# A linear-attention and GELU-MLP kernel: kv of a batch in one slot, batch 4 loaded before batch 2's x transposes, maps and casts behind the n slots

## The chip, the cores and the metric

One NeuronCore of a Trainium2 chip runs the kernel. The metric is device time in microseconds (us). TensorE does the matmuls, VectorE, ScalarE and GpSimd the elementwise work, and SyncE (SP) issues nearly all DMAs; ScalarE issues the output writes.

## What is computed

q, k and v have 8 batches, 8 heads, 576 positions and a head size of 64. Each head goes through linear attention; its output x (4608 x 512) goes through two matrices with a tanh GELU between.

```python
phi = lambda x: np.where(x > 0, x, np.exp(x) - 1.0) + 1.0
q_p, k_p = phi(q), phi(k)
kv  = np.einsum('bhsd,bhse->bhde', k_p, v)
z   = np.sum(k_p, axis=2)
x   = np.einsum('bhsd,bhde->bhse', q_p, kv) / (np.einsum('bhsd,bhd->bhs', q_p, z)[..., None] + 1e-06)
x   = x.transpose(0, 2, 1, 3).reshape(4608, 512)
out = gelu_tanh(x @ w_in) @ w_out          # w_in 512 x 2048, w_out 2048 x 512
```

## The kernel before

**Tiling.** Of a batch's 576 positions, 512 ("main", four chunks of 128) are done by themselves; the remaining 64 of two batches are one "rest" tile of 128. So there are nine iterations of the MLP: iteration j (0 to 7) takes the 512 tokens of batch j, iteration 8 the rest tokens of all batches. An iteration has 16 `h` steps (four matmuls of 128x512 each, then a GELU by ScalarE into `g`) and 16 `o` steps (four matmuls each; four o steps fill one output tile).

**phi.** exp(x) comes from ScalarE (`exp_of`), max(x + 1, 1) from VectorE (`linear_of`, L223), and the minimum of the two from VectorE (`least_of`, L236). v is cast to bf16 beside a column of ones (`cast_v` L247, `cast_v_paired` L241, `cast_vr` L255), so that one matmul gives kv and z.

**Attention of a batch.** kv is summed on TensorE (`kv_main`, 40 matmuls, or `kv_paired`, 36, for batches 0 and 1) and copied into the block-diagonal `kvbd` (`kv_evac`). For each chunk c, `n` multiplies the transposed q (`qt`) with kvbd into PSUM (`n_ps`), and VectorE forms a reciprocal (L315) and a product (L317) that gives x (`nab`; `nab_in_banks` does the same in two halves with banks of its own). x is transposed to `xt`, which the h matmuls of that batch's iteration read: for batches 0 and 1 by TensorE and a ScalarE copy, for the others by DMA transposes that SP issues (L576). phi(q) is transposed likewise, by four DMA transposes per batch (L545) from batch 2 on. Each h matmul reads all four chunks of xt.

**PSUM.** Six banks (`bank`) rotate over h, o, t_ps and others; `pair_of_banks` is one more pair, with one buffer, which n uses for each chunk in turn.

**Order.** Each engine runs its instructions in the order in which the program writes them, and so does SP with its DMAs; an instruction that has to wait holds up what stands behind it. The program writes an iteration as 32 slots, one per step, with the work on later batches put into slots by hand: `at(j, slot, fn)` runs fn after that step of iteration j. Iterations 0 and from 2 on have h in slots 0 to 15 and o in 16 to 31; iteration 1 has h in 0 to 7, the first half of all four o tiles in 8 to 15, h in 16 to 23 and the second half of o in 24 to 31. `plan_prepare(b, s_linear, s_exp)` places the maps of q and k in the slots s_linear and +1, the casts of v in +2, the exponentials in s_exp, the minimum of q with its four DMA transposes in s_exp + 2 and that of k in + 4. `plan_attention(b, j, s_kv, s_n)` places kv, its evacuation, and n with the DMA transpose of each chunk. `plan_rest` does the rest tile; `load_batch(b)` issues q, k, on even b the rests of k and v (two DMAs each, for two batches), and v. Loads go into seven buffers of 1 MB that are used in turn.

First batch (batch 0) and second batch (batch 1) have programs of their own: `first_batch`, ahead of iteration 0, and `plan_second`, in iteration 0's o slots.

Of the kernel before, what the change touches and what calls it, by code (L numbers as in the profile page):

```python
# [15 lines left out]
def kernel(  # L16
# [15 lines left out]
    nc = tc.nc  # L32
# [3 lines left out]
    P = 128  # L36
# [40 lines left out]
    def pair_of_banks(name):  # L77
        return ps_a.tile([P, 2, 512], FP32, name=name, tag="a")
# [161 lines left out]
    def cast_v_paired(b, us, fn):  # L240
        fn(  # L241
            out=vp_paired(b)[:, :, us, 0:D].rearrange("p j u d -> p u j d"),
            in_=ld["v", b][:, us].rearrange("p u (j d) -> p u j d", d=D),
        )
# [9 lines left out]
            r = slice(REST * s, REST * (s + 1))  # L254
            nc.vector.tensor_copy(out=vrs[s][r, :, 0:D], in_=ld["vr", m][r])  # L255

    def kv_paired(b, ii, kv_ps):
        kp, vp = phi["k", b], vp_paired(b)
        for j in range(J):
            for a in range(2):  # L260
                r = slice(HP * a, HP * (a + 1))
                nc.tensor.matmul(  # L262
                    kv_ps[:, a, 2 * E * ii : 2 * E * (ii + 1)],
                    lhsT=kp[r, j, 2 * ii : 2 * ii + 2, :],
                    rhs=vp[r, j, 2 * ii : 2 * ii + 2, :],
                    start=(j == 0),
                    stop=(j == J - 1),
                    skip_group_check=True,
                )
# [13 lines left out]
                    skip_group_check=True,  # L283
                )

    def kv_evac(b, src, fns):
        for s, fn in enumerate(fns):
            r = slice(HP * s, HP * (s + 1))
            dst = kvbds[b % 4][r, :, E * s : E * (s + 1)]
            if b in PAIRED:  # L290
                fn(
                    out=dst.rearrange("p (a i) e -> p a i e", a=2),
                    in_=src[r, :, 0 : 4 * E].rearrange("p a (i e) -> p a i e", i=2)[
                        :, :, :, E * s : E * (s + 1)
                    ],
                )
            else:
                fn(out=dst, in_=src[r])  # L298

    def nab_mm(qt_c, kvbd, ns, rows=slice(0, P)):  # L300
        for i in range(NP):
# [23 lines left out]
    def nab(qt_c, b):  # L325
        n_ps = pair_of_banks("n_ps")
        nab_mm(qt_c, kvbds[b % 4], [n_ps[:, a] for a in range(2)])
        return nab_evac(n_ps, b in PAIRED)
# [56 lines left out]
    def first_batch():  # L385
        w_ps = bank("w_ps", [P, 512])

        def keep_warm(n):
            for _ in range(n):
                nc.tensor.matmul(w_ps, lhsT=warm[:, 0:P], rhs=warm)  # L390

        qt = pt.tile([P, C, NP, P], BF16, name="qt")
        qs = (slice(0, 4), slice(4, 8))

        def transpose_q(s, fn):
            t_ps = bank("t_ps", [P, C, 2, P], BF16)
            for i in range(2):
                for c in range(C):
                    h = 4 * s + 2 * i
                    nc.tensor.transpose(  # L400
                        t_ps[:, c, i, :], phi["q", 0][:, c, h : h + 2, :], ident
                    )
            fn(out=qt[:, :, 2 * s : 2 * s + 2, :], in_=t_ps)

        keep_warm(18)
        for s in range(2):
            exp_of("q", 0, qs[s])
            exp_of("k", 0, halves[s])
            linear_of("q", 0, qs[s])
            least_of("q", 0, qs[s])  # L410
            linear_of("k", 0, halves[s])
            least_of("k", 0, halves[s])
        transpose_q(0, nc.vector.tensor_copy)
        keep_warm(10)
        transpose_q(1, nc.scalar.copy)
        cast_v_paired(0, halves[0], nc.vector.tensor_copy)
        cast_v_paired(0, slice(2, 3), nc.scalar.copy)
        cast_v_paired(0, slice(3, 4), nc.vector.tensor_copy)
        keep_warm(2)
        kv_ps = pair_of_banks("kv_ps")  # L420
        for ii in range(2):
            kv_paired(0, ii, kv_ps)
        kv_evac(0, kv_ps, (nc.vector.tensor_copy, nc.scalar.copy))
        gelu_table()
        for s in range(2):
            cast_w_in(0, nc.gpsimd.tensor_copy, slice(256 * s, 256 * s + 256))
        for i in range(1, 4):
            cast_w_in(i, nc.gpsimd.tensor_copy)
        for i in range(2):
            cast_w_out(i, nc.gpsimd.tensor_copy)  # L430
        cast_w_out(2, nc.gpsimd.tensor_copy, slice(0, 2))
        keep_warm(2)

        xts[0] = pt.tile([P, NP, MAIN], BF16, name="xt")
        x = {0: nab_in_banks(qt[:, 0], 0), 1: nab(qt[:, 1], 0)}
        for c in range(C):
            transpose_x(x[c], xt_chunk(0, c), nc.scalar.copy)
            if c + 2 < C:
                x[c + 2] = (nab_in_banks, nab)[c % 2](qt[:, c + 2], 0)
            if c > 0:  # L440
                h_quarter(0, c - 1, 3)
        h_quarter(0, C - 1, 3)
# [15 lines left out]
    def plan_second():  # L458
        b = 1
        x = {}  # L460

        def maps():
            for n in "qk":
                exp_of(n, b)
            gelu_table()
            for n in "qk":
                linear_of(n, b)
                least_of(n, b)
            cast_w_out(2, nc.vector.tensor_copy, slice(2, 4))

        def transpose_q():
            qts[b] = pt.tile([P, C, NP, P], BF16, name="qt")
            for s in range(2):
                t_ps = bank("t_ps", [P, 2, NP, P], BF16)
                for c in range(2):
                    for i in range(NP):
                        nc.tensor.transpose(
                            t_ps[:, c, i, :],
                            phi["q", b][:, 2 * s + c, 2 * i : 2 * i + 2, :],
                            ident,  # L480
                        )
                nc.scalar.copy(qts[b][:, 2 * s : 2 * s + 2], t_ps)

        def casts():
            cast_v_paired(b, halves[0], nc.vector.tensor_copy)
            cast_v_paired(b, halves[1], nc.scalar.copy)

        def kv():
            kv_ps = pair_of_banks("kv_ps")
            for ii in range(2):  # L490
                kv_paired(b, ii, kv_ps)
            kv_evac(b, kv_ps, (nc.vector.tensor_copy, nc.scalar.copy))
            cast_w_out(3, nc.scalar.copy, slice(0, 1))
            cast_w_out(3, nc.vector.tensor_copy, slice(1, 2))
            cast_w_out(3, nc.gpsimd.tensor_copy, slice(2, 4))

        def n(c):
            x[c] = nab(qts[b][:, c], b)

        def t(c):  # L500
            if c == 0:
                xts[b] = pt.tile([P, NP, MAIN], BF16, name="xt")
            transpose_x(x[c], xt_chunk(b, c), nc.scalar.copy)

        at(0, 15, maps)
        at(0, 23, transpose_q)
        at(0, 25, casts)
        at(0, 27, kv)
        at(0, 27, n, 0)
        at(0, 28, n, 1)  # L510
        at(0, 28, t, 0)
        at(0, 29, n, 2)
        at(0, 29, t, 1)
        at(0, 30, h_quarter, b, 0, 2)
        at(0, 30, n, 3)
        at(0, 30, t, 2)
        at(0, 31, h_quarter, b, 1, 2)
        at(0, 31, t, 3)
        at(0, 31, h_quarter, b, 2, 2)
        at(0, 31, h_quarter, b, 3, 2)  # L520
# [41 lines left out]
        at(j, s + 4, least_k)  # L562

    def plan_attention(b, j, s_kv, s_n):
        box = {}

        def kv(i):
            if i == 0:
                box["kv"] = bank("kv_ps", [P, NP, E])
            kv_main(b, i, box["kv"])  # L570

        def n(c):
            x = nab(qts[b][:, c], b)
            if c == 0:
                xts[b] = pt.tile([P, NP, MAIN], BF16, name="xt")
            nc.sync.dma_start_transpose(out=xt_chunk(b, c), in_=x)  # L576

        for i in range(NP):
            at(j, s_kv[i], kv, i)
        at(j, s_kv[-1], lambda: kv_evac(b, box["kv"], (nc.vector.tensor_copy,) * 2))  # L580
        for c in range(C):
            at(j, s_n[c], n, c)

# [110 lines left out]
    plan_second()  # L694
    plan_prepare(2, (1, 2), (1, 7))
    at(1, 7, gelu_table)
    plan_attention(2, 1, (16, 17, 18, 19), (20, 21, 23, 24))
    plan_prepare(3, (1, 11), (1, 23))
    plan_rest(0, 1, 23, 28, 2, 14)
    at(1, 23, gelu_table)  # L700
    at(1, 26, load_batch, 4)
    for b in range(4, B):
        plan_prepare(b, (b - 2, 8), (b - 2, 15))
        if b > 4:
            at(b - 3, 15, load_batch, b)
    for m in range(1, 4):
        at(2 * m - 1, 14, load_rest, "qr", q, m)
        plan_rest(m, 2 * m, 15, 22, 2 * m + 1, 14)
    for b in range(4, B):
        at(b - 2, 15, gelu_table)  # L710
    for b in range(3, B):
        plan_attention(b, b - 1, (1, 2, 3, 4), (6, 8, 10, 12))

    for j in range(B + 1):
        iteration(j)
# [30 lines left out]
```

## Time and profile before

| | |
|---|---|
| runs, median (lowest to highest) | 317.26 us (316.98 to 318.13) |
| profiled execution: time, span | 317.26 us, 315.5 us |
| busy share of the span: TensorE, VectorE, ScalarE, GpSimd | 91%, 34%, 52%, 6% |
| mean granted clock of TensorE | 0.984 |
| chain that ended last, by engine | PE 67%, DMA 13%, DVE 12%, ACT 3% |
| bytes moved, mean rate | 53.76 MB, 170 GB/s |

In the profile PE is TensorE's matmul queue, PEld its weight loads, DVE is VectorE, ACT ScalarE, POOL GpSimd, SPq and ACTq the instructions that issue DMAs. L302 is line 302 of the kernel. The chain that ended last is followed back from the last instruction, at each step to what released it. A busy share is a mean over stages with different limits, so the stages are to be read one by one.

### The profile page before, as it was taken

How to read it: one execution, taken by the hardware profiler on the slowest of the kernel's cores; microseconds unless marked ns; L12 is line 12 of the kernel's file. 1: busy time of each engine (PE TensorE's matmuls, PEld its weight loads, DVE VectorE, ACT ScalarE, POOL GpSimd, SP SyncE). 2: the span in 40 equal slices, each digit the busy share in tenths (PEclk: the TensorE clock that was granted, in tenths of full speed). 3: DMA queues.
4: the chain of work that ended last, by engine and by line, in shares of the span. 5: the costliest groups of instructions: out<-in, count | busy, mean ns of one | idle time of the engine just before them, and what ended most of it. 6: DMA issues, size and time to landing. Idle time of an engine off the chain costs nothing.

```text
span 315.5 us, 4408 instructions
## 1 busy us (share of the span) xinstructions
PE 287.8 (91%) x1796; PEld 138.1 (44%) x1796; DVE 108.1 (34%) x178; ACT 163.6 (52%) x221; POOL 18.4 (6%) x25
## 2 busy tenths in 40 slices
PE   8699978998997099999998799999999999999995
PEld 3364445444443044454443344444444444444444
DVE  3731448374625425064304650463032100200001
ACT  4666944783954048366634492558257146206600
POOL 5164310000000000000000000000000000000000
PEclk9999999999999679999999999999999999999999
DMA  7999998953399929915896299134402210011022
GB/s 262 409 406 402 407 359 271 369 134 67 68 215 320 166 50 320 262 54 66 273 312 132 50 328 273 30 57 95 155 19 50 85 66 0 19 66 66 0 64 71
DMA packets 71379, 53.76 MB, mean 170 GB/s; under 512 B 42048, under 2 KB 62784, under 8 KB 71360
## 3 DMA queue, kind: packets, MB, share of 16 engines
q1 hardware_dynamic: 68656, 44.58, 49.5%
q10 hardware_dynamic: 2704, 8.91, 8.6%
q8 instruction: 14, 0.23, 0.3%
q14 instruction: 5, 0.04, 0.1%
HBM read 36.70 MB, written 9.44 MB: 146 GB/s over the span
## 4 chain that ended last, share of the span: by engine, by line
PE 67%; DMA 13%; DVE 12%; ACT 3%; issue 2%; SPq 1%; DVEq 0%
PE o_ps L642 32%; PE h_ps L357 30%; DMA k_x<-in_k_dram 7%; DMA qt<-q_p 3%; DVE x L317 3%; DMA qtr<-qr_p 2%; PE n_ps L302 2%; DVE k_p L223 2%; DVE q_p L223 2%; PE kv_ps L277 1%; DVE vp L247 1%; ACT g L367 1%; DVE r L315 1%; DVE k_p L236 1%; PE kv_ps L262 1%
## 5 line engine op out<-in xcount | busy, mean ns | idle before, releaser
L642 PE MATMUL o_ps<-w_out_sb,g 128*128 128x512 bf16 (+1 forms) x592 | 127.1, 373 | 1.4 <-DVE w_out_sb L143 1.1
L357 PE MATMUL h_ps<-xt,w_in_sb 128*128 128x512 bf16 (+1 forms) x572 | 123.2, 360 | 2.2 <-ACT g L367 1.6
L367 ACT ACTIVATE g<-h_ps 128x512 bf16<-128x512 f32 x144 | 85.1, 597 | 71.3 <-PE h_ps L357 70.1
L642 PEld LDWEIGHTS <-g 128*128 128x128 bf16 x592 | 57.6, 98 | 66.7 <-issue 1.8
L357 PEld LDWEIGHTS <-w_in_sb 128*128 128x128 bf16 x636 | 56.6, 98 | 58.6 <-issue 3.9
L615 ACT COPY o_sb<-o_ps 128x512 f32<-128x512 f32 (+1 forms) x18 | 10.3, 574 | 60.1 <-PE o_ps L642 53.4
L613 DVE COPY o_sb<-o_ps 128x512 f32<-128x512 f32 (+1 forms) x19 | 12.8, 675 | 59.5 <-PE o_ps L642 59.5
L302 PE MATMUL n_ps<-kvbd,qt 128*128 128x130 bf16 x128 | 12.7, 223 | 16.6 <-DVE x L317 13.9
L317 DVE TENSOR_TENSOR x<-n_ps,r 128x512 bf16<-128x512 f32 x34 | 23.5, 692 | 1.2
L236 DVE TENSOR_TENSOR q_p<-q_p,q_e 128x2048 bf16<-128x2048 bf16 (+1 forms) x9 | 10.0, 1107 | 32.1 <-ACT q_e L212 32.0
L302 PEld LDWEIGHTS <-qt 128*128 128x128 bf16 x128 | 9.3, 99 | 25.3 <-issue 18.6
L315 DVE RECIPROCAL r<-n_ps 128x8 f32<-128x8 f32 x34 | 7.0, 206 | 38.5 <-PE n_ps L302 38.4
L298 DVE CAST kvbd<-kv_ps 64x260 bf16<-64x260 f32 x12 | 5.1, 427 | 41.3 <-PE kv_ps L277 41.2
L212 ACT ACTIVATE q_e<-q_x 128x2048 bf16<-128x2048 f32 (+1 forms) x9 | 15.5, 1721 | 3.0 <-DMA q_x<-in_q_dram 3.0
L212 ACT ACTIVATE k_e<-k_x 128x2048 bf16<-128x2048 f32 (+2 forms) x9 | 15.8, 1755 | 0.8 <-DMA k_x<-in_k_dram 0.8
L223 DVE TENSOR_SCALAR q_p<-q_x 128x2048 bf16<-128x2048 f32 (+1 forms) x9 | 9.9, 1102 | 15.5 <-DMA q_x<-in_q_dram 15.5
L357 PE MATMUL h_ps<-xt_rest,w_in_sb 128*128 128x512 bf16 x64 | 14.0, 379 | 0.0
L223 DVE TENSOR_SCALAR k_p<-k_x 128x2048 bf16<-128x2048 f32 (+2 forms) x9 | 11.0, 1224 | 1.4 <-DMA k_x<-in_k_dram 1.4
L390 PE MATMUL w_ps<-warm 128*128 128x512 bf16 x32 | 9.7, 460 | 1.2 <-DVE warm L177 1.2
L236 DVE TENSOR_TENSOR k_p<-k_p,k_e 128x2048 bf16<-128x2048 bf16 (+2 forms) x9 | 10.2, 1136 | 1.5 <-ACT k_e L212 1.1
L381 ACT ACT_TABLE_LOAD x8 | 10.3, 1283 | 0.1
L212 ACT ACT_TABLE_LOAD x8 | 10.3, 1283 | 0.1
(51 smaller groups left out, 100.9 us busy)
## 6 DMA issues: line engine op xcount, KB each, us to landing
out_dram<-o_sb ACTq DMA_DIRECT2D x16, 512.0 KB, 4.3
q_x<-in_q_dram SPq DMA_DIRECT2D x6, 1024.0 KB, 6.8
k_x<-in_k_dram SPq DMA_DIRECT2D x6, 1024.0 KB, 9.4
v_x<-in_v_dram SPq DMA_DIRECT2D x6, 1024.0 KB, 8.4
w_st<-in_moe_w_in_dram SPq DMA_DIRECT2D x4, 1024.0 KB, 13.8
w_st<-in_moe_w_out_dram SPq DMA_DIRECT2D x4, 1024.0 KB, 13.5
q_x<-in_q_dram SPq DMA_DIRECT2D x4, 512.0 KB, 8.7
k_x<-in_k_dram SPq DMA_DIRECT2D x2, 576.0 KB, 5.8
```

The costliest lines, as they stand in the source:

```text
L212: nc.scalar.activation(by_chunk(exps[name, b], hs), x[:, hs].rearrange("p h (c d) -> p h c d", d=D), AF.Exp,)
L223: nc.vector.tensor_scalar(by_chunk(phi[name, b], hs), x[:, hs].rearrange("p h (c d) -> p h c d", d=D), 1.0, 1.0, op0=ALU.add, op1=ALU.max,)
L236: nc.vector.tensor_tensor(p, p, e, op=ALU.min)
L302: nc.tensor.matmul(ns[i // 2][rows, 2 * E * (i % 2) : 2 * E * (i % 2 + 1)], lhsT=qt_c[:, i, rows], rhs=kvbd[:, i, :], skip_group_check=True,)
L315: nc.vector.reciprocal(r, n_v[:, :, :, D])
L317: nc.vector.tensor_tensor(x_view(x, paired), n_v[:, :, :, 0:D], r[:, :, :, None].to_broadcast([P, 2, NP, D]), op=ALU.mult,)
L357: nc.tensor.matmul(h_ps[:, ts], lhsT=w_in_sb[:, c, P * m : P * (m + 1)], rhs=xt[:, c, ts], start=(c == 0), stop=(c == KM - 1), skip_group_ ...
L367: nc.scalar.activation(g[:, m, :], h_ps, AF.Gelu_apprx_tanh)
L381: nc.scalar.preload_act_table_set("gelu_apprx_tanh_and_others")
L613: nc.vector.tensor_copy(dst, src)
L615: nc.scalar.copy(dst, src)
L642: nc.tensor.matmul(o_ps, lhsT=g[:, m, P * t : P * (t + 1)], rhs=w_out_sb[:, m, fs], start=(m == 0), stop=(m == MM - 1),)
```

## The change

kv of batches 2 to 7 is done in one slot instead of four, in `pair_of_banks`, and is evacuated right there. n of batches 3 to 7 moves from slots 6, 8, 10, 12 to 4, 6, 8, 10, and that of batch 2 from 20, 21, 23, 24 to 18 to 21. The maps and casts of batches 4 to 7 move from slots 8 to 10 to 13 to 15, those of batch 3 by one slot. Batch 4's load moves from slot 26 of iteration 1 to slot 10, the later loads from 15 to 18, the loads of q's rests from 14 to 18, and the rests' n from 14 to 12. For batches 0 and 1 the evacuation of kv is split by PSUM bank instead of by partition half, and casts and copies change engine or order. The core of the diff:

```diff
@@ kv_evac @@
-    def kv_evac(b, src, fns):
-        for s, fn in enumerate(fns):
...
+    def kv_evac(b, blocks, src, fn):
+        for s in range(2):
+            r, es = slice(HP * s, HP * (s + 1)), slice(E * s, E * (s + 1))
+            fn(out=kvbds[b % 4][r, blocks, es], in_=src[r, :, es] if b in PAIRED else src[r])
@@ first_batch @@
-        transpose_q(0, nc.vector.tensor_copy)
+        transpose_q(0, nc.scalar.copy)
         keep_warm(10)
         transpose_q(1, nc.scalar.copy)
-        cast_v_paired(0, halves[0], nc.vector.tensor_copy)
-        cast_v_paired(0, slice(2, 3), nc.scalar.copy)
-        cast_v_paired(0, slice(3, 4), nc.vector.tensor_copy)
         keep_warm(2)
-        kv_ps = pair_of_banks("kv_ps")
         for ii in range(2):
-            kv_paired(0, ii, kv_ps)
-        kv_evac(0, kv_ps, (nc.vector.tensor_copy, nc.scalar.copy))
+            cast_v_paired(0, halves[ii], nc.vector.tensor_copy)
+            kv_ps = [bank("kv_ps", [P, 2 * E]) for _ in range(2)]
+            kv_paired(0, ii, lambda a, ii: kv_ps[a])
+            for a, fn in enumerate((nc.vector.tensor_copy, nc.scalar.copy)):
+                block = slice(2 * a + ii, 2 * a + ii + 1)
+                kv_evac(0, block, kv_ps[a].rearrange("p (i e) -> p i e", i=1), fn)
...
-        x = {0: nab_in_banks(qt[:, 0], 0), 1: nab(qt[:, 1], 0)}
+        x = {0: nab(qt[:, 0], 0), 1: nab_in_banks(qt[:, 1], 0)}
@@ plan_second @@
-                least_of(n, b)
+            least_of("q", b)
             cast_w_out(2, nc.vector.tensor_copy, slice(2, 4))
+            least_of("k", b)
...
-            kv_evac(b, kv_ps, (nc.vector.tensor_copy, nc.scalar.copy))
+            for a, fn in enumerate((nc.vector.tensor_copy, nc.scalar.copy)):
+                src = kv_ps[:, a, 0 : 4 * E].rearrange("p (i e) -> p i e", i=2)
+                kv_evac(b, slice(2 * a, 2 * a + 2), src, fn)
+
+        def last_w_out():
             cast_w_out(3, nc.scalar.copy, slice(0, 1))
...
-        at(0, 27, kv)
+        at(0, 26, kv)
+        at(0, 26, last_w_out)
@@ plan_attention @@
+        def kv():
+            kv_ps = pair_of_banks("kv_ps")[:, 0, 0 : NP * E].rearrange("p (i e) -> p i e", e=E)
+            for i in range(NP):
+                kv_main(b, i, kv_ps)
+            kv_evac(b, slice(0, NP), kv_ps, nc.vector.tensor_copy)
...
-        for i in range(NP):
-            at(j, s_kv[i], kv, i)
-        at(j, s_kv[-1], lambda: kv_evac(b, box["kv"], (nc.vector.tensor_copy,) * 2))
+        at(j, s_kv, kv)
@@ the plan @@
-    plan_attention(2, 1, (16, 17, 18, 19), (20, 21, 23, 24))
-    plan_prepare(3, (1, 11), (1, 23))
-    plan_rest(0, 1, 23, 28, 2, 14)
+    plan_attention(2, 1, 16, (18, 19, 20, 21))
+    at(1, 10, load_batch, 4)
+    plan_prepare(3, (1, 12), (1, 23))
+    plan_rest(0, 1, 23, 28, 2, 12)
     at(1, 23, gelu_table)
-    at(1, 26, load_batch, 4)
     for b in range(4, B):
-        plan_prepare(b, (b - 2, 8), (b - 2, 15))
+        plan_prepare(b, (b - 2, 13), (b - 2, 15))
         if b > 4:
-            at(b - 3, 15, load_batch, b)
+            at(b - 3, 18, load_batch, b)
     for m in range(1, 4):
-        at(2 * m - 1, 14, load_rest, "qr", q, m)
-        plan_rest(m, 2 * m, 15, 22, 2 * m + 1, 14)
+        at(2 * m - 1, 18, load_rest, "qr", q, m)
+        plan_rest(m, 2 * m, 15, 22, 2 * m + 1, 12)
...
-        plan_attention(b, b - 1, (1, 2, 3, 4), (6, 8, 10, 12))
+        plan_attention(b, b - 1, 2, (4, 6, 8, 10))
```

## Rows read from the trace of the kernel before

**Rows 1.** Windows, iterations 2 to 6: stretch, its length, TensorE busy, clock, DMA, GB/s.

```profile
86.64:129.71 43.07, 32.86 (x194) 0.88 0.90 217
129.71:161.00 31.29, 30.73 (x194) 1.00 0.67 172
161.00:194.45 33.45, 30.43 (x186) 1.00 0.81 203
194.45:225.74 31.29, 30.73 (x193) 1.00 0.38 92
225.74:255.84 30.10, 30.10 (x185) 1.00 0.19 58
```

**Rows 2.** Timeline, iteration 2: start, length, work, [idle before <- what ended it].

```profile
100.13 0.39 PE L302 MATMUL n_ps<-kvbd,qt 128*128 128x130 bf16 x4 [1.82 <-DVE x L317]
...
107.51 1.23 DVE L247 CAST vp<-v_x 128x2048 bf16<-128x2048 f32 x1 [4.61 <-DMA v_x<-in_v_dram]
...
110.64 0.59 PE L302 MATMUL n_ps<-kvbd,qt 128*128 128x130 bf16 x4 [8.38 <-DVE x L317]
```

**Rows 3.** Timeline of SP's DMA issues (the length is the issue's).

```profile
72.12 1.28 SPq L118 DMA_DIRECT2D qr<-in_q_dram  x2
76.81 6.14 SPq L576 DMA_TRANSPOSE xt<-x  x4
...
90.53 0.83 SPq L100 DMA_DIRECT2D q_x<-in_q_dram  x1
...
150.06 0.61 SPq L100 DMA_DIRECT2D q_x<-in_q_dram  x1
```

**Rows 4.** Windows, TensorE alone, about the fall and return of the clock.

```profile
104.00:106.00 2.00, 0.00 (x0) 0.64 2.21 292
114.00:116.00 2.00, 2.00 (x15) 0.80 0.01 0
```

**Rows 5.** Chain that ended last, first batch: start, length, work.

```profile
11.07 0.60 DVE qt L403
```

**Rows 6.** Timeline, first batch.

```profile
11.59 1.42 DVE L241 CAST vp<-v_x 128x1152 bf16<-128x1152 f32 x2
...
12.40 1.34 PE L262 MATMUL kv_ps<-vp,k_p 64*128 64x130 bf16 x36 [1.52 <-DVE vp L241]
...
14.31 0.37 ACT L291 CAST kvbd<-kv_ps 64x260 bf16<-64x260 f32 x1 [1.78 <-DVE kvbd L291]
```

**Rows 7.** Timeline, TensorE in the last slots of iteration 0.

```profile
41.62 3.18 PE L642 MATMUL o_ps<-w_out_sb,g 128*128 128x512 bf16 x14 [1.11 <-DVE w_out_sb L143]
...
46.93 0.40 PE L302 MATMUL n_ps<-kvbd,qt 128*128 128x130 bf16 x4 [0.99 <-ACT kvbd L291]
```

**Rows 8.** Timeline, slots 17 to 21 of iteration 1.

```profile
69.39 1.02 PE L357 MATMUL h_ps<-xt,w_in_sb 128*128 128x512 bf16 x4 [0.41 <-ACT g L367]
...
70.37 1.22 DVE L247 CAST vp<-v_x 128x2048 bf16<-128x2048 f32 x1
...
71.10 1.02 PE L357 MATMUL h_ps<-xt,w_in_sb 128*128 128x512 bf16 x4 [0.41 <-ACT g L367]
...
76.89 0.39 PE L302 MATMUL n_ps<-kvbd,qt 128*128 128x130 bf16 x4 [0.25 <-DVE x L317]
```

**Rows 9.** Chain, iteration 6: slots with kv, and two slots of h.

```profile
228.88 0.28 PE kv_ps L277 x10
229.16 0.97 PE h_ps L357 x4
...
233.72 1.73 PE h_ps L357 x8
```

**Rows 10.** Chain: DMA transposes from issue to landing.

```profile
100.73 7.86 DMA qtr<-qr_p
...
159.66 10.25 DMA qt<-q_p
```

**Rows 11.** Tile views: landing of qt issued from 165 to 167, of xt from 81 to 83.

```profile
DMA to landing us min/median/max: 5.2/5.7/6.2
...
DMA to landing us min/median/max: 2.3/2.3/2.4
```

More of the change, by code (lines that the diff above doesn't have):

```diff
@@ L255, in cast_vr, with kv_paired @@
             nc.vector.tensor_copy(out=vrs[s][r, :, 0:D], in_=ld["vr", m][r])
-    def kv_paired(b, ii, kv_ps):
+    def kv_paired(b, ii, kv_of):
         kp, vp = phi["k", b], vp_paired(b)
@@ L262, in kv_paired @@
                 nc.tensor.matmul(
-                    kv_ps[:, a, 2 * E * ii : 2 * E * (ii + 1)],
+                    kv_of(a, ii),
                     lhsT=kp[r, j, 2 * ii : 2 * ii + 2, :],
@@ L284, in kv_main @@
                 )
-    def kv_evac(b, src, fns):
-        for s, fn in enumerate(fns):
[L288 to L298, printed above, removed]
+    def kv_evac(b, blocks, src, fn):
+        for s in range(2):
+            r, es = slice(HP * s, HP * (s + 1)), slice(E * s, E * (s + 1))
+            fn(out=kvbds[b % 4][r, blocks, es], in_=src[r, :, es] if b in PAIRED else src[r])
     def nab_mm(qt_c, kvbd, ns, rows=slice(0, P)):
@@ L438, in first_batch @@
             if c + 2 < C:
-                x[c + 2] = (nab_in_banks, nab)[c % 2](qt[:, c + 2], 0)
+                x[c + 2] = (nab, nab_in_banks)[c % 2](qt[:, c + 2], 0)
             if c > 0:
@@ L490, in kv @@
             for ii in range(2):
-                kv_paired(b, ii, kv_ps)
-            kv_evac(b, kv_ps, (nc.vector.tensor_copy, nc.scalar.copy))
+                kv_paired(b, ii, lambda a, ii: kv_ps[:, a, 2 * E * ii : 2 * E * (ii + 1)])
+            for a, fn in enumerate((nc.vector.tensor_copy, nc.scalar.copy)):
+                src = kv_ps[:, a, 0 : 4 * E].rearrange("p (i e) -> p i e", i=2)
+                kv_evac(b, slice(2 * a, 2 * a + 2), src, fn)
+        def last_w_out():
             cast_w_out(3, nc.scalar.copy, slice(0, 1))
@@ L564, in plan_attention @@
     def plan_attention(b, j, s_kv, s_n):
[L565 to L570, printed above, removed]
+        def kv():
[3 more added lines that the diff above has]
+            kv_evac(b, slice(0, NP), kv_ps, nc.vector.tensor_copy)
         def n(c):
```

## The prediction

> **What bounds the kernel now.** I read the windows cut at the iterations first, then the timeline of the worst of them, then SP's queue. The windows [rows 1] give each iteration's length and TensorE's busy time in it. Iteration 6 has no idle time: 30.10 us, all busy. Iterations 3 and 5 have 0.56 us of idle time each, iteration 4 has 3.02, and iteration 2 is 43.07 us long with 10.21 idle and a mean clock of 0.88. So TensorE is the bound everywhere and most of what can be had lies in iteration 2. There the timeline [rows 2] shows n matmuls that wait for VectorE's x, 1.82 and 8.38 us. VectorE was not busy: its cast of v, in its queue ahead of the n slot's reciprocal, waited 4.61 us for batch 4's v. That load's first DMA was issued at 90.53 [rows 3] and v landed as the cast began, at 107.51: 17.0 us for q, k, both rests and v. The granted clock fell to half meanwhile [rows 4]: its mean of 0.64 over 104 to 106 puts the fall at 104.6, and 0.80 over 114 to 116 puts the return at 114.8. TensorE had work from 110.64 on, so 4.15 us of it ran at 1.2 instead of 2.4 GHz: 2.1 us lost.
>
> The profiled execution has a span of 315.5 us and a time of 317.26, which is also the median of the runs; the sum is made against 317.26.
>
> **The change part by part.**
>
> *First batch.* VectorE loses the first qt copy (0.60 us on the chain, [rows 5]), so its first cast of v starts at 11.07. But the cast of the second half now stands behind the evacuation of the first half's kv, which waits for TensorE. From [rows 6]: the two casts (a half and a quarter) took 1.42, so a half is some 0.8; 36 kv matmuls took 1.34, so a half is 0.67; one evacuation by ScalarE took 0.37, and two quarter-size copies on one engine are taken at 0.42, with 0.1 for the handover. 11.07 + 0.8 + 0.67 + 0.52 + 0.8 + 0.67 + 0.52 = 15.05, against 14.68 (14.31 + 0.37) now: **+0.4**. The copies of 64x65 are not in the trace; if they cost next to nothing the part is -0.4, if each costs as much as a 0.37 copy it is +1.0. The swap of the two n forms moves the same VectorE work about: nothing. The second qt copy on ScalarE ends before kv needs it.
>
> *Iteration 0.* o at slot 24 waits 1.11 us for VectorE's cast of w_out, behind both minima; now it goes ahead of the second minimum. kv moves from slot 27 to 26, so one o step lies between kv and n, where TensorE now waits 0.99 us for the evacuation [rows 7]; the cast of the last w_out part moves behind the evacuation, with TensorE's next use a slot later. Both waits go: **-2.1**. If only the first goes: -1.1.
>
> *Iteration 1.* Four accumulators of o and kv_ps leave one bank to h, so h waits 0.41 us for each GELU [rows 8] and a slot takes 1.71 us (69.39 to 71.10 in the pattern; four such slots), where iteration 6 shows 0.28 + 0.97 = 1.25 with kv in it [rows 9]. kv_ps now sits in the pair of banks that n uses: 4 x 0.46 = -1.84. kv in one slot: four slots at 1.25 against 0.865 without kv (1.73 for two slots) cost 1.54; 4 x 0.28 + 0.1 in one place is 1.22, so -0.33. Against that, n(0) comes sooner and VectorE is still at batch 3's maps: its cast of v ends at 71.59 [rows 8], the evacuation ends some 0.9 us later, and TensorE would be ready at 71.6: +0.9. With n in adjacent slots there are three waits for x of 0.25 [rows 8] where there are two: +0.25. Sum **-1.0**, between -2.2 (nothing new waits) and 0.
>
> *Batch 4's load.* It goes from behind batch 3's q transposes to behind batch 2's, where SP is free at 72.12 [rows 3]. All buffers that it takes have been read by then. What is moved behind it on SP: batch 2's four x transposes (at 76.81 now), the rest of q, batch 3's q transposes. Two traces show what that costs. Where transposes stand behind a load they landed after it: the one issued at 100.73 took 7.86 us, to 108.6, 18.1 after its load began at 90.53; those behind the load that began at 150.06 were issued from 159.66, the first landed at 169.9 [rows 10], the last, issued at 165.8, at 171.0 [rows 11], 21 after the load's start. The second load had two output writes beside it and the first still had transposes in flight; the new place has no output writes. I take 18 for the last of four: 72.12 + 18 = 90.1. Iteration 1 ends at 86.64, less 1.0: 85.6. Every h matmul reads all four chunks, so iteration 2 begins with a **wait of 4.5 us** that is not there now (parts 1 and 2 move both ends alike). With 21 it is 7.5; by SP's issue alone (9.6 for the load as at 150.06; 4.6 until the fourth transpose goes out, three of the four in the 6.14 at 76.81 [rows 3]; 2.3 to land, as the batch's last two did [rows 11]) it is 16.5 and 3.0. During such a wait the clock can fall as it did in iteration 2; I take the same loss, **+2.1**, between 0 (the clock holds) and twice that.
>
> *Iterations 2 to 6.* Batch 4 is there when VectorE comes to it, and the maps and casts go to slots 13 to 15, behind all n slots (4, 6, 8, 10). q transposes go ahead of the next load on SP. So no n waits for a load, a map or a q transpose. A clean iteration is 30.10 - 0.33 = 29.77, and one with a rest's n, by the busy time of 3 and 5, 30.73 - 0.33 = 30.40 (2, 3 and 5 have one). Against [rows 1]: iteration 2 -12.67, 3 -0.89, 4 -3.68, 5 -0.89, 6 -0.33, together **-18.5**. Merging kv is 1.65 of this; if it saves nothing, the part is -16.8. n has two slots per step, 1.73 us of h alone [rows 9], and in iteration 6, with the same spacing and no map between, it waits for nothing [rows 1]. What is late next: the loads start some slots later, behind the q transposes. With 17.0 us to land, a load with rests that begins 26 us into an iteration ends 13 into the next, where its v is wanted at slot 15, 14.6 us in. Nothing is in VectorE's queue behind it then but minima and o copies; were it late by more than these 1.6 us, the minimum of q and its transposes would be as late, and they are not read before the next iteration's slot 4.
>
> Sum: 0.4 - 2.1 - 1.0 + 4.5 + 2.1 - 18.5 = -14.6, and 317.3 - 14.6 = **302.7**.
>
> **The rivals.**
>
> *No wait at iteration 2.* If SP issues the load as fast as two rests at 72.12 (0.64 each, [rows 3]; 7 x 0.64 = 4.5), and transposes land 2.3 after issue whatever is ahead, the last is there at 72.12 + 4.5 + 1.3 (the rest of q) + 4.6 + 2.3 = 84.8, before 85.6. Both are needed. Time: 302.7 - 4.5 - 2.1 = 296.1. Against it: in [rows 10] neither holds. The Trainium skill ("DMA: Bandwidth & Descriptors", section on queues, rings and completion order) has a rule for this side: descriptors are taken in order on each DMA engine, but DMAs of one issuing engine need not complete in order. The trace rather shows the order kept; by the rule with SP's issue time as it is, the wait would be 3.0 and the sum 301.2.
>
> *A longer wait.* Behind the load as at 150.06: a wait of 7.5 us, 305.7. For it: SP took 9.6 us to issue that load, so it issues slowly while much is in flight. Against it: no output writes there.
>
> *The pace doesn't come.* Merging kv saves nothing and an n waits once per iteration as in iterations 3 and 5 now (0.56): 302.7 + 1.65 + 5 x 0.56 = 307.2. This is the case in which the regrouping doesn't do what it says.
>
> *Slower than before.* The new order makes a ring: load, cast of v, minimum of q, four q transposes on SP, next load. With 17.0 + 1.2 + about 1.2 + 6.1 it takes 25.5 us and hides in an iteration of 30.1. From 4.6 us more on it sets the pace of iterations 3 to 6, and with 14.6 / 4 = 3.7 beyond that, a load of 25.3 us, all the gain is gone: 318 and more. No load in the trace comes near it.
>
> **How the numbers follow.** Chances: forecast with a wait of 3 to 6 us 0.48 (its own range 300 to 305); no wait 0.17; longer wait 0.2; pace not had 0.1; the ring 0.03; the rest 0.02 for what is not seen. The range goes from the no-wait case with the first batch's lower bound, about 295, to 307.5, past the longer wait and the missing pace. A measurement of this kernel tells about 0.5% from no change, 1.6 us. Faster by more 0.95, within it 0.02, slower 0.03.
>
> **What would show it.** Right: no wait of n for x above 0.5 us in iterations 2 to 6 and 29.7 to 30.5 us for each; h of iteration 2 starts with a wait of 3 to 6 us put down to the xt transposes, with half the clock around it; batch 4's v lands some 15 us after its load began; no h waits for a GELU in slots 17 to 20 of iteration 1; the waits of 1.11 and 0.99 in iteration 0 are gone; n of the first batch starts near 15.0. Wrong: xt of batch 2 lands before iteration 1 ends (then 296), or q of batch 3, now the last on SP, lands after iteration 2's slot 4 and its n waits again.

## The result and the profile after

The changed kernel takes 301.82 us (median of 4 executions, 301.46 to 302.74) where the kernel before, timed beside it, takes 317.12 (316.36 to 318.13): a ratio of 0.952, 95% interval 0.949 to 0.955. The forecast was 302.7. The profiled execution took 301.89 us with a span of 300.1, so the spans differ by 15.4 us.

The page of the changed kernel: the share of TensorE, its busy tenths and granted clock in 40 slices, and the engines of the chain that ended last.

```profile
PE 283.5 (94%) x1796; PEld 138.1 (46%) x1796; DVE 108.5 (36%) x181; ACT 164.5 (55%) x225; POOL 19.1 (6%) x25
...
PE   8789998997939999999999999999999999999995
...
PEclk9999999999987999999999999999999999999999
...
PE 85%; DMA 5%; DVE 4%; ACT 2%; issue 2%; SPq 0%; DVEq 0%; ACTq 0%
```

TensorE had 91% and has 94%; its share of the chain went from 67% to 85%. One dip is left in the busy row, the slice that begins at 82.5 us, and the granted clock is below full in it and the next. The waits of TensorE between 22 and 285 us (who waited for whom: total, times, longest; three of 0.6, 0.4 and 0.2 us are left out) name it:

```profile
PE h_ps L348 <- DMA xt<-x: 4.9, 1, 4.9
PE n_ps L293 <- DVE kvbd L289: 1.2, 1, 1.2
PE n_ps L293 <- DVE x L308: 1.1, 4, 0.3
```

The waits for VectorE's x of [rows 2] are gone; the largest is the new wait for the x transposes, at the start of iteration 2. Windows of the changed kernel (stretch, its length; busy time of PE, PEld, DVE, ACT and POOL, each with its number of instructions; clock, DMA, GB/s): iteration 1, the wait behind it, iterations 2 to 6, and the stretch of half clock.

```profile
50.04:84.40 34.36, 31.82 (x225) 15.84 (x223) 18.95 (x28) 24.16 (x30) 0.00 (x0) 1.00 0.94 284
84.40:89.45 5.05, 0.17 (x2) 0.03 (x1) 2.13 (x5) 1.91 (x3) 0.00 (x0) 0.82 1.02 280
...
89.45:121.81 32.36, 32.36 (x193) 14.79 (x193) 14.65 (x25) 17.46 (x23) 0.00 (x0) 0.92 0.37 90
121.81:151.70 29.89, 29.89 (x193) 14.27 (x192) 12.47 (x19) 17.00 (x22) 0.00 (x0) 1.00 0.71 186
151.70:181.13 29.43, 29.43 (x186) 14.09 (x185) 13.76 (x23) 18.04 (x24) 0.00 (x0) 1.00 0.77 204
181.13:211.02 29.89, 29.89 (x193) 14.29 (x192) 12.47 (x19) 17.00 (x22) 0.00 (x0) 1.00 0.67 183
211.02:240.44 29.42, 29.42 (x185) 14.08 (x184) 6.59 (x14) 12.64 (x20) 0.00 (x0) 1.00 0.20 59
87.65:94.48 6.83, 5.03 (x12) 1.61 (x12) 0.00 (x0) 1.19 (x2) 0.00 (x0) 0.50 0.61 194
```

Iterations 2 to 6 hold no idle time at all. Iteration 1 of before, in the same view, is the one row needed beside [rows 1]:

```profile
51.55:86.64 35.09, 32.40 (x225) 16.36 (x224) 19.93 (x30) 24.97 (x31) 0.00 (x0) 1.00 0.59 176
```

The sum of the prediction against these rows. Iteration 1 is cut at 84.40, where TensorE would have begun iteration 2: in a kernel below that has no such wait, it takes 34.37 us. For the clock, iteration 2 is set against the 29.89 us of an undisturbed iteration with a rest's n.

| step | predicted | measured, before to after |
|---|---|---|
| first batch and iteration 0 | +0.4 - 2.1 = -1.7 | -1.5 (iteration 1 begins at 50.04, not 51.55) |
| iteration 1 | -1.0 | -0.7 (35.09 to 34.36) |
| wait for xt at iteration 2 | +4.5 | +5.0 (84.40 to 89.45) |
| half clock there | +2.1 | +2.5 (32.36 less 29.89) |
| iterations 2 to 6 | -18.5 | -20.7 (13.18 + 1.40 + 4.02 + 1.40 + 0.68) |
| sum | -14.6 | -15.4 |

### The profile page after: what moved, and what is told of

Read it like the earlier page. It is cut to its first block, busy times and chain, and to the rows that moved or that the text cites. A ratio compares the mean times of both kernels' runs of the same rounds, so it can differ in the third digit from the quotient of the medians.

```text
span 300.1 us, 4430 instructions
## 1 busy us (share of the span) xinstructions
PE 283.5 (94%) x1796; PEld 138.1 (46%) x1796; DVE 108.5 (36%) x181; ACT 164.5 (55%) x225; POOL 19.1 (6%) x25
## 4 chain that ended last, share of the span: by engine, by line
PE 85%; DMA 5%; DVE 4%; ACT 2%; issue 2%; SPq 0%; DVEq 0%; ACTq 0%
PE h_ps L348 41%; PE o_ps L636 38%; DMA k_x<-in_k_dram 4%; PE n_ps L293 2%; PE kv_ps L277 2%; DMA xt<-x 1%; ACT k_e L212 1%; PE kv_ps L262 1%; DVE o_sb L607 1%; DVE q_p L223 1%; DVE k_p L236 1%; DVE vp L241 0%; DVE x L308 0%; ACT L212 0%; PE t_ps L340 0%
## 5 line engine op out<-in xcount | busy, mean ns | idle before, releaser
L348 PE MATMUL h_ps<-xt,w_in_sb 128*128 128x512 bf16 (+1 forms) x572 | 121.2, 362 | 5.4 <-DMA xt<-x 4.9
L348 PEld LDWEIGHTS <-w_in_sb 128*128 128x128 bf16 x636 | 57.7, 98 | 65.8 <-issue 8.8
L609 ACT COPY o_sb<-o_ps 128x512 f32<-128x512 f32 (+1 forms) x18 | 10.3, 574 | 60.1 <-PE o_ps L636 53.3
L289 DVE CAST kvbd<-kv_ps 64x260 bf16<-64x260 f32 (+2 forms) x18 | 6.6, 367 | 38.1 <-PE kv_ps L277 33.3
L223 DVE TENSOR_SCALAR k_p<-k_x 128x2048 bf16<-128x2048 f32 (+2 forms) x9 | 10.2, 1131 | 4.5 <-DMA k_x<-in_k_dram 4.5
L212 ACT ACT_TABLE_LOAD x8 | 10.3, 1283 | 0.1
L372 ACT ACT_TABLE_LOAD x8 | 10.3, 1283 | 0.1
```

The source lines that it names most:

```text
L212: nc.scalar.activation(by_chunk(exps[name, b], hs), x[:, hs].rearrange("p h (c d) -> p h c d", d=D), AF.Exp,)
L223: nc.vector.tensor_scalar(by_chunk(phi[name, b], hs), x[:, hs].rearrange("p h (c d) -> p h c d", d=D), 1.0, 1.0, op0=ALU.add, op1=ALU.max,)
L348: nc.tensor.matmul(h_ps[:, ts], lhsT=w_in_sb[:, c, P * m : P * (m + 1)], rhs=xt[:, c, ts], start=(c == 0), stop=(c == KM - 1), skip_group_ ...
L372: nc.scalar.preload_act_table_set("gelu_apprx_tanh_and_others")
L609: nc.scalar.copy(dst, src)
```

## The experiments

Each was timed in one of three sets beside the kernel before, which took 314.91, 315.81 and 315.51 us (medians) in them. The ratio is that to before, and the brackets hold its 95% interval. The edits are of the changed kernel ("after") if nothing else is said. After itself was repeated in the second set, with 300 to 302 us expected: 303.1 us, 0.959 (0.956 to 0.961).

### The load at its old place

```diff
-    at(1, 10, load_batch, 4)
+    at(1, 26, load_batch, 4)
```

> The changed kernel with batch 4's load alone put back to slot 26 of iteration 1, behind batch 2's x and batch 3's q transposes. Theory (what frees iteration 2 is that the maps and casts stand behind the n slots; the early load only costs a wait): the wait of 4.9 us for xt at iteration 2 and the 2.6 us of half clock go, nothing comes in their place: about 294.3 us. VectorE's cast of batch 4's v then waits some 5 us near 100 to 106, with no n behind it. Rival (the early load is what frees iteration 2): TensorE waits again for batch 4's v, in iteration 2's n or o or in iteration 3's first n, some 5 to 10 us: 299 to 305 us.

Measured: 305.79 us, 0.9705 (0.964 to 0.977). My theory, that the early load only costs (294.3), fell: without it the kernel is no faster. TensorE waits again, as the rival had it, but not for batch 4's v. Its profiled execution also has a fall of the clock in the first batch that the profiles of after don't have (last section, some 2 us), so the traces compare the two better: iterations 1 and 2 take 18.24 + 38.99 us from iteration 1's h of slot 16 on, against 23.28 + 32.36 in after, 1.6 less. SP's queue in this kernel, the landing of the two DMAs of interest (median us from issue), and TensorE's timeline:

```profile
99.71 1.42 SPq L100 DMA_DIRECT2D v_x<-in_v_dram  x1
101.24 1.70 SPq L585 DMA_TRANSPOSE qtr<-qr_p  x1
...
v_x<-in_v_dram SPq DMA_DIRECT2D x1, 1024.0 KB, 6.6
qtr<-qr_p SPq DMA_TRANSPOSE x1, 6.2
...
107.43 0.65 PE L293 MATMUL n_ps<-kvbd,qtr 128*64 128x130 bf16 x8 [7.71 <-DMA qtr<-qr_p]
```

The wait for xt is gone as expected. But the transpose of the rest queries (qtr), which was of no account before, stands behind the load on SP: v landed at 99.71 + 6.6 = 106.3, qtr at 107.4, and the rest's n, now at slot 12, waits 7.71 us for it, with half the clock from 103.46 to 110.29. Where the prediction asked what is late next in iterations 2 to 6, it named q's transposes and not this one.

### The moved maps alone, the moved load alone

Both are edits of the kernel before.

```diff
-        plan_prepare(b, (b - 2, 8), (b - 2, 15))
+        plan_prepare(b, (b - 2, 13), (b - 2, 15))
```

> The kernel before with only the maps and casts of batches 4 to 7 moved from slots 8 to 10 to 13 to 15. Theory: n's waits for VectorE in iterations 2 to 5 go (8.4 + 1.8 in iteration 2 with 2.1 of half clock, about 0.5, 1.8 and 0.5 in 3 to 5), the wait for q's transposes in iteration 4 (1.2) stays: about 317.1 - 15.1 = 302.0 us, with no wait at the start of iteration 2. Rival (the late load still holds TensorE up somewhere else): 307 to 314 us.

```diff
+    at(1, 10, load_batch, 4)
     plan_prepare(3, (1, 11), (1, 23))
...
-    at(1, 26, load_batch, 4)
```

> The kernel before with only batch 4's load moved from slot 26 to slot 10 of iteration 1. Theory: iteration 2's waits for v go (10.2 and 2.1 of half clock), iteration 2 begins with a wait for xt of about 5 us and 2.5 of half clock, the rest is as before: about 317.1 - 12.3 + 7.5 = 312.3 us. Rival (the early load is most of the gain): 305 us or less.

Measured: maps alone 308.55 us, 0.9802 (0.974 to 0.986), faster by about 2%; load alone 315.08, 1.001 (0.997 to 1.005), no change. TensorE's waits, the first kernel's largest, then the second's three largest:

```profile
PE n_ps L302 <- DMA qtr<-qr_p: 4.1, 1, 4.1
```

```profile
PE n_ps L302 <- DVE x L317: 5.5, 7, 1.8
PE h_ps L357 <- DMA xt<-x: 4.0, 1, 4.0
PE n_ps L302 <- DMA qt<-q_p: 2.8, 1, 2.8
```

Maps behind the n slots take n off batch 4's v, and the rest's n then waits for qtr behind the load, as in the first experiment. The early load alone takes away the 8.38 us of [rows 2] and gives all of it back: 4.0 for xt, 2.8 for q's transposes two iterations on, and n still stands behind maps and casts. So the theory for the maps alone (302.0) fell and its rival (307 to 314) held; for the load alone the rival (305 or less) is out, and the theory's 312.3 took both waits of [rows 2] off, but the one of 1.8 us stays, and the wait for q's transposes grows from 1.2 us to 2.8. The parts don't add: -6.2 and 0 us, against about -15 for the change.

### The clock kept up during the wait

```diff
+    def warm_wait(n):
+        w_ps = bank("w_ps", [P, 512])
+        for _ in range(n):
+            nc.tensor.matmul(w_ps, lhsT=warm[:, 0:P], rhs=warm)
+
+    at(1, 31, warm_wait, 20)
```

> The changed kernel with 20 matmuls of 128x512 on zeros at the end of iteration 1, 4.3 us of work inside the wait of 4.9. They add work and give nothing to the output. Theory (the wait is for data, the half clock is a cost of its own): the wait's end stays at about 89.4, the clock stays at full speed, h in iteration 2 runs at the usual pace: about 2.6 us less, 299.2 us. Rival (the clock falls for another reason, or the work only delays h): 301.8 us or more.

Measured: 301.05 us, 0.957 (0.950 to 0.964). TensorE's timeline of this kernel, and then that of the repeat of after:

```profile
84.42 4.48 PE L711 MATMUL w_ps<-warm 128*128 128x512 bf16 x20
91.10 2.75 PE L348 MATMUL h_ps<-xt,w_in_sb 128*128 128x512 bf16 x11 [2.21 <-issue]
```

```profile
91.34 4.88 PE L348 MATMUL h_ps<-xt,w_in_sb 128*128 128x512 bf16 x12 [6.52 <-DMA xt<-x]
```

With TensorE at work for 4.48 us of the wait, the clock stays full and iteration 2 takes 29.89 us (32.03 in the repeat of after). So the clock's 2.1 to 2.5 us is a cost of its own beside the wait. The time itself doesn't show it: 0.957 lies between after's 0.952 and its repeat's 0.959, and the theory's 299.2 was missed, because the x transposes landed at 91.0 here, not 89.4. The repeat of after waited 6.52 us. The wait is thus 4.9 to 6.5 us from execution to execution; the forecast's 3 to 6 was a little narrow.

### The load behind the rest's transposes

```diff
-    at(1, 10, load_batch, 4)
+    at(1, 29, load_batch, 4)
```

> The changed kernel with batch 4's load in slot 29 of iteration 1, one place further back than with slot 26: behind the transpose of q's rest, too. Theory (with slot 26 the wait was for that transpose alone, queued behind the load on SP; VectorE's late cast of v holds nothing up): neither the wait for xt at iteration 2 nor that for the rest's n remains, some 7 us less than the changed kernel. Rival (a load this late holds TensorE up anyway, by VectorE's cast, the o copies or the next q transposes): within 2 us of the changed kernel or slower.

Measured: 295.74 us, 0.937 (0.932 to 0.942), 7.4 us less than the repeat of after beside it. There is no wait at iteration 2, which takes 29.90 us, and none for a qtr in it. This is the test of the mechanism found in the first experiment: what matters is which transposes stand behind the load on SP. The same thing is left once, an iteration later. SP's queue, and TensorE's largest wait:

```profile
117.35 1.09 SPq L100 DMA_DIRECT2D v_x<-in_v_dram  x1
118.54 6.73 SPq L585 DMA_TRANSPOSE qtr<-qr_p  x1
```

```profile
PE n_ps L293 <- DMA qtr<-qr_p: 1.7, 1, 1.7
```

### The load in another queue

Batch 4's load is issued by GpSimd instead of SP, at slot 10 still:

```diff
...
-    at(1, 10, load_batch, 4)
+    at(1, 10, load_batch, 4, nc.gpsimd)
```

> The changed kernel with batch 4's load (the same DMAs in the same slot) issued from GpSimd instead of SP. Theory (the x transposes of batch 2 wait for SP's issue of the load and behind its packets in SP's queue): they are issued from about 72 and the last lands by about 81, the wait at iteration 2 goes, some 7 us less than the changed kernel. Rival (the DMA engines are full, whichever queue the load is in): the last x transpose lands within 2 us of now, and the wait stays at 3 us or more.

Measured: 301.03 us, 0.951 (0.947 to 0.956), 2.1 us less than the repeat of after. GpSimd, with little in its queue, issued q at 46.74 and the others from 61.72 to 71.05, where SP does so from 70.53 to 78.76 in after, and the load met batch 2's q transposes. Of this kernel TensorE's timeline in iteration 1 and the landing of these four transposes, issued from 66.76 on, and then their landing in after:

```profile
75.68 0.62 PE L293 MATMUL n_ps<-kvbd,qt 128*128 128x130 bf16 x4 [5.78 <-DMA qt<-q_p]
...
qt<-q_p SPq DMA_TRANSPOSE x4, 8.5
```

```profile
qt<-q_p SPq DMA_TRANSPOSE x4, 2.8
```

They took 8.5 us (median) instead of 2.8. xt was in time, but the wait (5.8 and 0.6) and the half clock (74.02 to 80.85) had only moved to n of iteration 1. Theory (7 us less) and rival (the wait stays) both missed, since q's transposes paid in place of x's. So a load in another queue can delay transposes on SP as well. What was ahead of them on SP was late, too: batch 3's v landed at 71.7 and the last of q's rests at 74.3 (66.0 and 66.7 in after), and the first transpose landed 1.4 us behind them, at 75.7. Whether the load slowed the transposes themselves or the DMAs ahead of them in SP's queue, and what its earlier start did, this run doesn't tell apart. The Trainium skill ("DMA: Bandwidth & Descriptors", section on issuing engines not being separate DMA queues) says that DMAs of all issuing engines run on the same 16 DMA engines and interleave. The trace agrees so far that a load issued by GpSimd went with 8.5 instead of 2.8 us for SP's transposes.

### kv in three slots again

For batches 3 to 7, kv is done in slots 0, 1 and 2 (one, one and two of its four parts of ten matmuls), still in `pair_of_banks`:

```diff
...
-        at(j, s_kv, kv)
+        parts = ((0,), (1,), (2, 3)) if b > 2 else ((0, 1, 2, 3),)
+        for n_part, heads in enumerate(parts):
+            at(j, s_kv - len(parts) + 1 + n_part, kv_part, heads)
```

> The changed kernel with kv of batches 3 to 7 in three slots (heads 0 and 1, 2 and 3, 4 to 7, in slots 0, 1 and 2) instead of one; nothing else moves. Theory by the changed kernel's trace (40 matmuls in one place cost 0.76 us where four groups of ten cost 1.54, so each change between h and kv costs about 0.23): two more groups per batch, 0.45 us per iteration, 2.3 us in all. Rival (my sum, 0.11 per change): 0.22 per iteration, 1.1 us in all.

Measured: 305.74 us, 0.967 (0.963 to 0.970), 2.6 more than the repeat of after. The chain that ended last in iteration 3 (start, us, what), in after and in this kernel:

```profile
121.97 2.59 PE h_ps L348 x12
124.56 0.76 PE kv_ps L277 x40
125.32 1.83 PE h_ps L348 x8
```

```profile
124.38 0.86 PE h_ps L348 x4
125.24 0.28 PE kv_ps L277 x10
125.52 0.97 PE h_ps L348 x4
...
127.74 0.44 PE kv_ps L277 x20
```

Ten more kv matmuls without h between cost 0.44 - 0.28 = 0.16 us. A place of ten costs 0.28, and the four h behind it 0.97 instead of 0.865, together 0.385. So each stay at kv costs 0.23 us for the change of shape there and back, as the theory had it (2.3 us in all). Iterations 3 to 6 take 30.35, 29.88, 30.35 and 29.88: 0.45 or 0.46 more than in after, two more stays.

### The first batch as it was

`first_batch` of the kernel before in the changed kernel. (What was expected names batch 1 too; here only batch 0's order is put back.)

> After with the order of casts and copies of batches 0 and 1 put back as before. The sum of the prediction had that order at +0.4 us for the first batch; the traces agree (n starts at the same time though k landed 0.2 us earlier). My theory: 0.4 us less than the changed kernel, within what a measurement tells. Rival: the order brings a gain that the two traces hide, and the time is 0.5 to 1 us more.

Measured: 302.06 us, 0.958 (0.952 to 0.964). The change of the first batch is worth nothing that a time tells. In the traces the first h matmul of iteration 0 starts at 17.51 us here and at 17.81 in after: +0.3 for the new order, where the sum had +0.4; the repeat of after is itself 0.25 behind after here (iteration 1 begins at 50.29 and 50.04).

### The three leftovers together

The load at slot 29; the minimum and the transpose of the rest queries at slot 17, ahead of the next load at 18; and batch 1's kv in two banks instead of one pair:

```diff
-            kv_ps = pair_of_banks("kv_ps")
+            kv_ps = [bank("kv_ps", [P, 4 * E]) for _ in range(2)]
...
-    at(1, 10, load_batch, 4)
+    at(1, 29, load_batch, 4)
...
-        plan_rest(m, 2 * m, 15, 22, 2 * m + 1, 12)
+        plan_rest(m, 2 * m, 15, 17, 2 * m + 1, 12)
```

> After with batch 4's load at slot 29, behind iteration 1's last qtr, with the rests' minimum and qtr of iterations 1 and on one slot earlier (17, ahead of the later batches' load at 18 on SP), and with batch 1's kv in two single banks so that VectorE and ScalarE copy it out side by side. My theory (a qtr issued behind a load on SP lands with it; one pair of banks makes the two copies of kvbd run one after the other): no wait for qtr in iteration 3 (1.67 us with the load at 29 alone), and the n of iteration 0 that takes kvbd of batch 1 waits about 0.1 us for it and not 0.65. Time about 293.5 us where the load at 29 alone gave 295.7. Rival: minimum one slot earlier only waits for the queries' last half, and the wait moves to the batch's casts: within 1 us of the load at 29 alone.

The same with five unread matmuls in the first batch, behind the first half of kv:

```diff
             kv_paired(0, ii, lambda a, ii: kv_ps[a])
+            keep_warm(5 * (1 - ii))
```

> As the one before, with five matmuls whose result nobody reads between the first batch's two halves of kv, where TensorE waits 1.4 us for a cast. My theory: the early fall of the clock (14.7 to 21.5 us) that some executions of other kernels here show follows that idle time; with it filled the clock stays full over the first batch, the time is that of the one before or up to 1 us less (about 293), and its executions lie closer together. Rival: the fall has another cause; the same time, or 0.2 us more for the five matmuls.

Measured: 293.75 us (293.59 to 296.13), 0.932 (0.925 to 0.940), and 293.73 (293.64 to 294.1), 0.930 (0.925 to 0.935): both beat the two kernels of this study. Against the load at 29 alone (0.937, 0.932 to 0.942) the intervals overlap, so what the other two edits bring is read from the traces. In the first kernel, iterations 2 and 3 take 29.89 and 29.90 us and no wait of TensorE behind the first batch is above 1.2 us. Copying kvbd of batch 1 out of PSUM, in after and in this kernel:

```profile
44.12 0.60 DVE L289 CAST kvbd<-kv_ps 64x130 bf16<-64x130 f32 x2 [3.13 <-PE kv_ps L262]
...
44.82 0.54 ACT L289 CAST kvbd<-kv_ps 64x130 bf16<-64x130 f32 x2 [1.95 <-DVE kvbd L289]
...
45.42 0.39 PE L293 MATMUL n_ps<-kvbd,qt 128*128 128x130 bf16 x4 [0.44 <-ACT kvbd L289]
```

```profile
44.11 0.60 DVE L289 CAST kvbd<-kv_ps 64x130 bf16<-64x130 f32 x2 [3.12 <-PE kv_ps L262]
44.13 0.54 ACT L289 CAST kvbd<-kv_ps 64x130 bf16<-64x130 f32 x2 [1.25 <-PE kv_ps L262]
...
44.82 0.40 PE L293 MATMUL n_ps<-kvbd,qt 128*128 128x130 bf16 x4
```

With one tile for the pair of banks ScalarE's copy waits until VectorE's is done; with two tiles they run side by side and the wait is gone. The second kernel was meant to tell whether the clock's early fall (last section) follows TensorE's idle time in the first batch. None of its four executions lies above 294.1, one of the first's four does (296.13); four are too few to call it shown.

## Why the prediction was right, step by step

The forecast's case is what happened: n waits for nothing in iterations 2 to 6, the price is a wait for batch 2's xt at the start of iteration 2 with half the clock around it, and the load pays for itself. That 302.7 came within 0.9 us is in part luck: the first four rows of the table came out 1.4 us worse together than forecast, the last 2.2 better.

**First batch: right.** +0.4 was forecast; the traces with either order give +0.3, about as much as two executions differ.

**Iteration 0: a little too much.** The 1.11 us wait of [rows 7] is gone. Of the 0.99 us wait for kvbd 0.44 stays (0.66 in the repeat of after): the step that put one o matmul group between kv and n didn't see that the copies by VectorE and by ScalarE run one after the other, as they do in the first batch in [rows 6] (ScalarE's copy waited for VectorE's kvbd). Iteration 1 begins 1.5 us sooner and not 1.7.

**Iteration 1: right in its parts.** n(0) waits 1.2 us for VectorE's kvbd (0.9 forecast), n waits four times up to 0.3 for x, three of them here as forecast, and no h waits for a GELU. -0.7 against -1.0, and the 0.3 between them is n(0).

**The wait at iteration 2: right in size, by another path in part.** SP's queue of the changed kernel, with landing times of v and of the first x transpose, and the chain that ended last (the fourth x transpose):

```profile
70.53 0.52 SPq L100 DMA_DIRECT2D q_x<-in_q_dram  x1
...
77.72 1.04 SPq L100 DMA_DIRECT2D v_x<-in_v_dram  x1
78.87 1.47 SPq L572 DMA_TRANSPOSE xt<-x  x1
80.39 1.28 SPq L118 DMA_DIRECT2D qr<-in_q_dram  x2
81.77 4.89 SPq L572 DMA_TRANSPOSE xt<-x  x3
...
v_x<-in_v_dram SPq DMA_DIRECT2D x1, 1024.0 KB, 6.4
...
xt<-x SPq DMA_TRANSPOSE x1, 5.9
...
85.44 3.92 DMA xt<-x
...
89.45 5.22 PE h_ps L348 x12
```

The last transpose landed at 89.36, 18.8 us after the load began (18 taken, from [rows 10]). Iteration 1 ended at 84.40; the forecast's 85.6, moved by the -1.7 of the parts ahead of it, gives 83.9. The transposes of [rows 10] took 7.9 and 10.3 us to land behind their loads. The first x transpose here did the same: issued at 78.87, it took 5.9 us and landed 0.7 behind v (77.72 + 6.4 = 84.1). But the fourth, which ended the wait, was issued at 85.44, when the load had landed. SP's issuing of the load, of the rest of q and of three transposes took 14.9 of the 18.8 us, the landing of the fourth 3.9. The prediction's count by SP's issue alone had 9.6 + 4.6 and 2.3, 16.5 in all. So its 18 came out, but by a sum whose larger part is the issuing.

Of the rivals, no wait (296.1) failed on both its conditions: the load took SP 8.2 us to issue, and the transposes took more than 2.3 to land. No trace here shows a transpose that overtook a load ahead of it on SP: they landed 0.7, 1.1 (the first experiment) and 2.0 us (the load at 29: qtr, 118.54 + 12.9, against v, 117.35 + 12.1) behind v. The rule cited in the prediction from the Trainium skill ("DMA: Bandwidth & Descriptors", section on queues, rings and completion order), that DMAs of one issuing engine need not complete in order, forbids nothing of this. The longer wait (7.5) was nearly seen in the repeat, at 6.5.

**The clock: right.** The chain has 5.22 us for the first 12 h matmuls, at 1.2 GHz, and 2.59 in iteration 3 at 2.4: 2.6 us lost there, 2.5 over the iteration, for 2.1 forecast.

**Iterations 2 to 6: the mis-sized term.** -20.7 for -18.5. Two sizes were off. Merging kv was taken at -0.33 us per iteration, from 0.28 for each ten matmuls in one place and 0.1 for the change; the chain has 0.76 for all forty and 0.1 behind them, so it saves 30.10 - 29.42 = 0.68. That is 0.35 more than forecast, in five iterations 1.7 us. The 0.28 of [rows 9] is ten matmuls at 0.16 and a change of shape, and the change is paid once per place, not per ten. The other 0.5: a rest's n was priced at 30.73 - 30.10 = 0.63 from [rows 1] and costs 29.89 - 29.42 = 0.47 in each of three iterations. The rows of before held 0.16 us of matmul time that followed a wait, which was counted as work and went with the wait. The chain of before has both, n behind the 0.56 us wait of iteration 5 and n without a wait in iteration 6:

```profile
208.64 0.39 PE n_ps L302 x4
...
233.49 0.23 PE n_ps L302 x4
```

**The pace and the ring.** "The pace doesn't come" (307.2) is out, by five iterations without idle time; the ring that would have made it slower never closed, since each load hid in its iteration.

**What the prediction did not see** is where the early load's gain came from. It set the wait for xt against the wait for v, and never asked what else stood behind the load at its old place once the rest's n came at slot 12: with the maps moved, v at slot 26 holds nothing up any more, and qtr does. By the traces the early load buys 1.6 us over the old place (0.3 by the repeat, where its iterations take 24.92 + 32.03). The load at 29 is 7.4 us better than at 10: three slots behind its old place, with the iteration's last transposes ahead of it.

## What to carry to other kernels

When a large load is moved within a queue, list every transpose that will stand behind it, to the end of the next stage, and by when each is read. Of the three places tried here (slots 10, 26 and 29) the best was behind the last transpose that is read early, though the load itself then landed later. A waiting engine pays twice if its clock falls during the wait, so price both. Small matmuls of another shape were cheapest in one place here: count the places, not only the matmuls.

## What was not expected of the hardware

Each stay at the 128x65 kv matmuls between 128x512 h matmuls cost 0.23 us beside the matmuls. The Trainium skill ("TensorEngine Tiling (Array Packing)", section Key Properties) says that a change of tiling mode drains TensorE; it gives no time. In the traces kv runs with 128*64 tiles between 128*128 ones, and they agree in that the change has a price; that a drain is what takes the 0.23 us is not shown.

The clock fell to half in the first batch in the profiled executions of three kernels (the load at its old place, the moved maps alone, the load at 29) and not in those of others whose program is the same there. In the profiled execution of the kernel with the load at 29 (298.41 us; its three others took 294.78 to 296.18), this is the window:

```profile
14.77:21.60 6.83, 6.18 (x53) 5.37 (x53) 4.16 (x14) 3.32 (x6) 4.44 (x4) 0.50 1.05 405
```

TensorE had waited 1.16 and 1.42 us for VectorE's casts before the clock fell; the three-leftovers kernel waited as long (1.16 and 1.42) at the same place and its clock did not fall. What decides it is open.
